# A decode-attention kernel: the token mixer moved to GpSimd and spread over the head groups, the x layouts made from one row, the last chunk loaded step by step

## The chip, the cores and the metric

The kernel runs on one core of one Trainium2 chip. The metric is the device time of one execution in microseconds (us), lower is better; the profile's span is about 1.8 us shorter than this time (1303.5 against 1305.27 us for the profiled run of the kernel before). The program is on one core, so there is no second die to compare, and only fast runs are compared (a single run, whose state is unknown, is marked). The granted clock is the share of TensorE's full clock that the profile shows for a stretch.

## The reference, cut to what matters

One query token attends to a long cache. There are 16 query heads in 8 groups, 65536 keys of 256 numbers for each group, in bf16, so K and V together are 537 MB that have to be read once. Beside it runs a small token mixer (layer norm, a product that makes 1792 x 448 numbers, gelu, a sum back to 448), and a sigmoid gate mixes both.

```python
q = (x @ wq).reshape(B, Sq, 16, 256) ...          # x: 1 x 448
scores = einsum("bhqd,bhkd->bhqk", q, k) * (Dh ** -0.5)
o = einsum("bhqk,bhkd->bhqd", softmax(scores), v)  # then @ wo
u = gelu(einsum("bsd,sf->bdf", layernorm(x), w1) + b1)   # F = 1792
y = einsum("bdf,fs->bds", u, w2) + b2
return g * a + (1 - g) * b                         # g = sigmoid(sum(x * gate_w))
```

## The kernel before

K and V come in chunks of 4 MB (128 partitions x 32 KB) into a ring of five slots. A chunk is worked off in four steps, 256 steps in all. In a step, TensorE turns 1 MB of K in two halves, VectorE copies each half out of PSUM (where the results of TensorE's matmuls lie), TensorE makes scores, ScalarE takes exp, VectorE turns p, and four steps later TensorE multiplies p with V. The ring slot is then free and its next load is issued. The mixer rides along in the first head group, one block of 128 rows in every two steps.

```python
def mixer_mid(b):
    nc.vector.tensor_scalar(out=t_b[:], in0=t_b[:], scalar1=GELU_C1, scalar2=1.0, ...)   # L266
    nc.vector.tensor_tensor(out=t_b[:], in0=t_b[:], in1=u_b[:], op=ALU.mult)             # L269
    nc.scalar.activation(out=t_b[:], in_=t_b[:], func=ACT.Tanh, scale=GELU_C0)           # L270

def mixer_close(b):
    nc.vector.scalar_tensor_tensor(out=gel[:], in0=t_b[:], scalar=1.0, in1=u_b[:], ...)  # L273
    nc.tensor.matmul(y_ps, lhsT=w2T[:, b:b + 1], rhs=gel[:], ...)                        # L276
# ... cut: mixer_open makes u_b on VectorE (L260) and the square on ScalarE (L257)

for n in range(n_steps + LAG):          # LAG = 4
    transposes(n, 0); scores(n - 1); transposes(n, 1); p_transpose(n - 1)   # bounds cut
    mixer(n)                            # even n: close(b - 1), open(b); odd n: mid(b)
    epilogue(n)
    p_v(n - LAG)
    # ... cut: load the next K and V into the slots that are free now
```

In the timelines below each engine works its instructions in the order of the program. In an even step TensorE meets the matmul of `gel` directly after VectorE has been told to make `gel`, and VectorE does that only after the step's copies and the p transpose.

The x layouts before the change are several loads: `xa` (128 x 3), `xb` (2 x 64 x 1), the same for the gate weights, and a broadcast `xB` (128 x 448).

The softmax here doesn't subtract the row's maximum and nothing guards it: scores larger than these inputs give would overflow.

Of the kernel before, what the change touches and what calls it, by code (L numbers as in the profile page):

```python
# [8 lines left out]
FP32 = mybir.dt.float32  # L9
BF16 = mybir.dt.bfloat16  # L10
ACT = mybir.ActivationFunctionType
ALU = mybir.AluOpType
AXIS = mybir.AxisListType
# [3 lines left out]
DH = 256  # L17


NB = 64  # L20
CHUNK = 128 * NB

SB = 16
STEPS = NB // SB
RING = 5

LAG = 4
NPT = LAG + 2

GELU_C0 = 0.7978845608028654  # L30
GELU_C1 = 0.044715
# [3 lines left out]
def kernel(  # L35
# [15 lines left out]
    nc = tc.nc  # L51
    D = A_x.shape[-1]
    SK = A_k_cache.shape[2]
    F = B_w1.shape[-1]
    NF = F // 128
    KA = D // 128
    DA = KA * 128
# [3 lines left out]
    steps_g = n_chunks * STEPS  # L61
    n_steps = HKV * steps_g
    assert steps_g >= LAG + 4
    scale = 1.0 / (DH ** 0.5)
# [3 lines left out]
    const = ctx.enter_context(tc.tile_pool(name="const", bufs=1))  # L68
    ringp = ctx.enter_context(tc.tile_pool(name="ring", bufs=1))
    work = ctx.enter_context(tc.tile_pool(name="work", bufs=1))  # L70
    psum = ctx.enter_context(tc.tile_pool(name="psum", bufs=1, space=bass.MemoryType.PSUM))

    ring = [ringp.tile([128, NB * DH], BF16, name=f"ring{i}") for i in range(RING)]

    tps = [psum.tile([128, 8 * 128], FP32, name=f"tps{i}") for i in range(2)]
    sc = [psum.tile([128, 512], FP32, name=f"sc{i}") for i in range(2)]
    pv = psum.tile([128, 512], FP32, name="pv")
    misc = psum.tile([128, 512], FP32, name="misc")


    total = HKV * n_chunks
    LAST_K = [SB] * STEPS
    LAST_V = [2 * SB, SB, SB // 2 + 2, SB // 2 - 2]

    def load(item):
        i, is_v = divmod(item, 2)
        g, c = divmod(i, n_chunks)
        src = (A_v_cache if is_v else A_k_cache)[0, g, c * CHUNK:(c + 1) * CHUNK, :]
        src = src.rearrange("(p j) d -> p (j d)", j=NB)
        dst = ring[item % RING]  # L90
        parts = [NB]
        if i == total - 1:
            parts = LAST_V if is_v else LAST_K
        j = 0
        for n in parts:
            nc.sync.dma_start(out=dst[:, j * DH:(j + n) * DH], in_=src[:, j * DH:(j + n) * DH])
            j += n
# [4 lines left out]
    wqb = wq_slot[:, KA * HQ * DH:KA * HQ * DH + 8 * DH]  # L102
# [3 lines left out]
    for hh in range(2):  # L106
        nc.sync.dma_start(
            out=wqb[64 * hh:64 * hh + 64, :], in_=A_wq[DA:D, 8 * DH * hh:8 * DH * (hh + 1)]
        )
# [4 lines left out]
    xa = const.tile([128, KA], BF16)  # L114
    xb = const.tile([128, 2], BF16)
    gwa = const.tile([128, KA], BF16)
    gwb = const.tile([128, 1], BF16)
    nc.vector.memset(xb[:], 0.0)
    nc.vector.memset(gwb[:], 0.0)
    x_row = A_x[0, 0]  # L120
    nc.scalar.dma_start(out=xa[:], in_=x_row[0:DA].rearrange("(p k) -> p k", k=KA))
    for hh in range(2):
        nc.scalar.dma_start(
            out=xb[64 * hh:64 * hh + 64, hh:hh + 1], in_=x_row[DA:D].rearrange("(p o) -> p o", o=1)
        )
    nc.gpsimd.dma_start(out=gwa[:], in_=gate_w[0:DA].rearrange("(p k) -> p k", k=KA))
    nc.gpsimd.dma_start(out=gwb[0:64, :], in_=gate_w[DA:D].rearrange("(p o) -> p o", o=1))

    xB = work.tile([128, D], FP32, name="xB")
    nc.gpsimd.dma_start(out=xB[:], in_=x_row.partition_broadcast(128))  # L130
# [20 lines left out]
    ones_f = const.tile([128, 128], FP32)  # L151
    nc.gpsimd.memset(ones_f[:], 1.0)


    sel = const.tile([128, 2, 2], FP32)
    same = const.tile([128, 4, 32], FP32)
    nc.gpsimd.memset(sel[:], 0.0)
    nc.gpsimd.memset(same[:], 0.0)
    for a in range(4):
        nc.gpsimd.affine_select(  # L160
            out=sel[:].rearrange("p h r -> p (h r)"), in_=sel[:].rearrange("p h r -> p (h r)"),
            compare_op=ALU.not_equal, fill=1.0, base=-32 * a, pattern=[[-1, 4]],
            channel_multiplier=1,
        )
        for half in range(16):
            nc.gpsimd.affine_select(
                out=same[:, :, 2 * half:2 * half + 2], in_=same[:, :, 2 * half:2 * half + 2],
                compare_op=ALU.not_equal, fill=1.0, base=-32 * a, pattern=[[0, 4], [-16, 2]],
                channel_multiplier=1,
            )  # L170

# [8 lines left out]
    acc = work.tile([1, D], FP32, name="acc")  # L180
    res = work.tile([1, D], BF16, name="res")
# [4 lines left out]
    nc.vector.memset(pv[:], 0.0)  # L186


    xg = const.tile([128, KA + 1], FP32)
    nc.vector.tensor_tensor(out=xg[:, 0:KA], in0=xa[:], in1=gwa[:], op=ALU.mult)  # L190
    nc.vector.tensor_tensor(out=xg[:, KA:KA + 1], in0=xb[:, 0:1], in1=gwb[:], op=ALU.mult)
    xg1 = const.tile([128, 1], FP32)
    nc.vector.tensor_reduce(out=xg1[:], in_=xg[:], axis=AXIS.X, op=ALU.add)
    z_ps = misc[:, 500:501]
    nc.tensor.matmul(z_ps, lhsT=ones_f[:], rhs=xg1[:], start=True, stop=True)
# [5 lines left out]

    stats = const.tile([128, nc.vector.BN_STATS_DIM], FP32)
    nc.vector.bn_stats(out=stats[:], in_=xB[:])
# [4 lines left out]
    mhalf = const.tile([128, 1], FP32)  # L208
    nc.gpsimd.memset(mhalf[:], -0.5)
# [3 lines left out]
    for _ in range(2):  # L213
# [6 lines left out]
    h_bc = xB  # L220
    nc.vector.tensor_scalar(
        out=h_bc[:], in0=xB[:], scalar1=mv[:, 0:1], scalar2=rstd[:, 0:1],
# [7 lines left out]
    for c in range(2):  # L230
        for h in range(HQ):
            dst = q_ps[:, c * HQ + h:c * HQ + h + 1]
            for k in range(KA):
                nc.tensor.matmul(
                    dst, lhsT=wqa_v[:, k, h, :, c], rhs=xa[:, k:k + 1], start=(k == 0), stop=False
                )
            nc.tensor.matmul(
                dst, lhsT=wqb_v[:, h % 8, :, c], rhs=xb[:, h // 8:h // 8 + 1],
                start=False, stop=True,
            )  # L240
# [10 lines left out]
    y_ps = misc[0:1, 0:D]  # L251
    u_b = work.tile([128, D], FP32, name="u_b")
    t_b = work.tile([128, D], FP32, name="t_b")
    gel = work.tile([128, D], BF16, name="gel")

    def mixer_open(b):
        nc.scalar.activation(  # L257
            out=t_b[:], in_=h_bc[:], func=ACT.Square, scale=w1T[:, b:b + 1], bias=b1T[:, b:b + 1]
        )
        nc.vector.tensor_scalar(  # L260
            out=u_b[:], in0=h_bc[:], scalar1=w1T[:, b:b + 1], scalar2=b1T[:, b:b + 1],
            op0=ALU.mult, op1=ALU.add,
        )

    def mixer_mid(b):
        nc.vector.tensor_scalar(  # L266
            out=t_b[:], in0=t_b[:], scalar1=GELU_C1, scalar2=1.0, op0=ALU.mult, op1=ALU.add
        )
        nc.vector.tensor_tensor(out=t_b[:], in0=t_b[:], in1=u_b[:], op=ALU.mult)  # L269
        nc.scalar.activation(out=t_b[:], in_=t_b[:], func=ACT.Tanh, scale=GELU_C0)  # L270

    def mixer_close(b):
        nc.vector.scalar_tensor_tensor(  # L273
            out=gel[:], in0=t_b[:], scalar=1.0, in1=u_b[:], op0=ALU.add, op1=ALU.mult
        )
        nc.tensor.matmul(  # L276
            y_ps, lhsT=w2T[:, b:b + 1], rhs=gel[:], start=(b == 0), stop=(b == NF - 1)
        )

    def mixer_end():  # L280
        nc.vector.tensor_scalar(
            out=acc[:], in0=y_ps, scalar1=0.5, scalar2=b2[0:1, 0:1], op0=ALU.mult, op1=ALU.add
        )
        nc.vector.tensor_scalar(
            out=acc[:], in0=acc[:], scalar1=gate[0:1, 1:2], scalar2=None, op0=ALU.mult
        )

    mix_pitch = max(1, min(2, (steps_g + LAG - 2) // (NF + 1)))

    def mixer(n):  # L290
        if mix_pitch == 1:
            if n < NF:
                mixer_open(n)
                mixer_mid(n)
                mixer_close(n)
            if n == NF:
                mixer_end()
            return
        b, ph = divmod(n - 2, 2)
        if ph == 0:  # L300
            if 0 < b <= NF:
                mixer_close(b - 1)
            if b == NF:
                mixer_end()
            if 0 <= b < NF:
                mixer_open(b)
        elif 0 <= b < NF:
            mixer_mid(b)
# [47 lines left out]
    def den_tot(g):  # L356
        d_ps = misc[:, 501:502]
        nc.tensor.matmul(
            d_ps, lhsT=same[:].rearrange("p a m -> p (a m)"), rhs=dsum[:], start=True, stop=True
        )  # L360
        nc.vector.reciprocal(out=rden[:], in_=d_ps)
        nc.vector.tensor_tensor(out=rden[:], in0=rden[:], in1=gate[:, 0:1], op=ALU.mult)
# [6 lines left out]
    def o_turn(g):  # L369
        o_ps = misc[:, 504:508]  # L370
        for c in range(2):
            for half in range(2):
                lo = half * DH + c * 128
                nc.tensor.matmul(
                    o_ps[:, 2 * c:2 * c + 2], lhsT=pvs[:, lo:lo + 128], rhs=sel[:, half, :],
                    start=(half == 0), stop=(half == 1),
                )
        nc.vector.tensor_copy(out=oT[:], in_=o_ps)
# [85 lines left out]
```

## Time and profile before

| | before |
|---|---|
| time, median of the first 3 runs | 1303.32 us (1302.59 to 1304.16) |
| span of the profiled run | 1303.5 us |
| DMA rate, 112 to 230 us | 363 GB/s |
| DMA rate, 230 to 430 us | 432 GB/s |
| landing of the last-but-one K chunk | 1266.4 us |

The page's first two parts. Tenths and rates stand in 40 equal slices of the span, 32.6 us each.

```profile
PE 962.2 (74%) x8448; PEld 600.4 (46%) x8448; DVE 810.3 (62%) x897; ACT 194.7 (15%) x543; POOL 22.7 (2%) x94
...
DMA  9998889999999999999999999999999999999995
GB/s 358 428 421 377 370 354 383 430 432 429 430 432 431 432 433 433 431 432 431 431 433 429 432 432 430 432 430 434 431 432 432 430 433 432 432 433 431 429 429 251
```

No compute engine is near full over the span, and the loads run at 430 to 434 GB/s nearly everywhere. The exceptions are what can be won: the first slice, slices four to seven, and the end. The same in stretches of the span (length, busy time and instructions of each engine, granted clock, DMA share, GB/s; PE is TensorE and PEld its weight loads, DVE VectorE, ACT ScalarE, POOL GpSimd):

```profile
core 0: us, PE busy (x) PEld busy (x) DVE busy (x) ACT busy (x) POOL busy (x), PEclk, DMA share, GB/s
65.00:112.00 47.00, 34.32 (x260) 20.61 (x260) 31.65 (x41) 10.40 (x24) 0.00 (x0) 0.78 1.00 427
112.00:230.00 118.00, 92.19 (x760) 56.27 (x760) 84.55 (x108) 25.61 (x62) 0.00 (x0) 0.83 0.87 363
230.00:430.00 200.00, 149.60 (x1306) 93.18 (x1304) 121.75 (x128) 27.51 (x80) 1.50 (x2) 0.85 1.01 432
630.00:1030.00 400.00, 299.14 (x2627) 186.56 (x2626) 246.03 (x261) 55.71 (x162) 2.25 (x3) 0.85 1.00 432
```

From 112 to 230 us the DMA engines are busy only 0.87 of the time. The waits between 65 and 230 us (who waited for whom, total, times, longest) name the mixer, and the timeline (start, length, what) shows how:

```profile
ACT t_b L270 <- DVE t_b L269: 41.4, 12, 4.0
PE misc L276 <- DVE gel L273: 40.7, 13, 3.1
DVE kT_326 L317 <- PE tps_74 L316: 34.5, 14, 2.8
```

```profile
153.73 1.09 PE L316 MATMUL tps_75<-ident,ring_69 128*128 128x128 f32 x8
...
154.43 1.22 DVE L317 COPY kT_325<-tps_74 128x2048 bf16<-128x2048 bf16 x1
...
155.56 1.21 DVE L317 COPY kT_325<-tps_75 128x2048 bf16<-128x2048 bf16 x1
156.69 0.70 DVE L338 STREAM_TRANSPOSE pT_332<-p_328 128x512 bf16<-128x512 bf16 x1
157.32 0.58 DVE L273 SCALAR_TENSOR_TENSOR gel<-t_b,u_b 128x448 bf16<-128x448 f32 x1
157.93 0.51 DVE L260 TENSOR_SCALAR u_b<-xB,w1T,b1T 128x448 f32<-128x448 f32 x1
157.95 0.53 PE L276 MATMUL misc<-gel,w2T 128*1 128x448 bf16 x1 [3.13 <-DVE gel L273]
...
159.27 1.97 PE L316 MATMUL tps_74<-ident,ring_69 128*128 128x128 f32 x8
...
161.27 1.22 DVE L317 COPY kT_326<-tps_74 128x2048 bf16<-128x2048 bf16 x1 [2.83 <-PE tps_74 L316]
```

TensorE stands still for 3.13 us until `gel` is there. Only then does it turn the next K half, and VectorE in its turn stands still for 2.83 us. The two engines take turns instead of overlapping. From one matmul of `gel` to the next it is 11.0 to 12.4 us, while the 4 MB of a pair come every 9.8 us (half of the 19.67 us between K chunks later on). So ring slots come free too late, and the loads have to wait for them.

The end is another matter. In the chain of work that ended last, the last-but-one K chunk lands at 1242.58 + 23.80 = 1266.4 us; from there eight steps of 3.13 us and the closing arithmetic take 37 us:

```profile
1242.58 23.80 DMA ring_73<-in_A_k_cache_dram
```

### The profile page before, as it was taken

The page shows a single profiled execution, that of the slowest core. Times are in us where ns is not written, and L with a number is a line of the kernel's source. Part 1 is how long each engine was busy: PE and PEld are TensorE (multiplying, and loading weights), DVE is VectorE, ACT ScalarE, POOL GpSimd, SP SyncE. Part 2 cuts the span into 40 slices and gives each one's busy share as a digit, 9 for nine tenths or more (in the row PEclk, how much of TensorE's full clock was granted, in tenths as well). Part 3 has the DMA queues.
Part 4 walks back from the last instruction along what each step waited for, and adds up shares of the span by engine and source line. Part 5 has one row for each costly group of instructions (what it writes and reads, how often), then busy time and mean ns, then how long its engine had stood idle before and what let it go on. Part 6 is the DMA issues. An engine that isn't in the chain of part 4 may idle for free.

```text
span 1303.5 us, 19519 instructions
## 1 busy us (share of the span) xinstructions
PE 962.2 (74%) x8448; PEld 600.4 (46%) x8448; DVE 810.3 (62%) x897; ACT 194.7 (15%) x543; POOL 22.7 (2%) x94
## 2 busy tenths in 40 slices
PE   3577778776777876867876876867877867868778
PEld 2344445444444444544544544544544544445444
DVE  2666668655655756656656656646556646657557
ACT  0122221111111111111111111111111111111111
POOL 5000000000000000000000000000000000000000
PEclk9777789888978878888888888889888878888889
DMA  9998889999999999999999999999999999999995
GB/s 358 428 421 377 370 354 383 430 432 429 430 432 431 432 433 433 431 432 431 431 433 429 432 432 430 432 430 434 431 432 432 430 433 432 432 433 431 429 429 251
DMA packets 21575, 545.71 MB, mean 419 GB/s; under 512 B 3057, under 2 KB 3314, under 8 KB 4466
## 3 DMA queue, kind: packets, MB, share of 16 engines
q1 hardware_dynamic: 19602, 540.55, 96.9%
q0 software_dynamic: 1584, 3.92, 0.8%
q8 instruction: 66, 1.08, 0.3%
q14 instruction: 19, 0.16, 0.0%
q10 hardware_dynamic: 304, 0.00, 0.0%
HBM read 544.34 MB, written 0.00 MB: 418 GB/s over the span
## 4 chain that ended last, share of the span: by engine, by line
DMA 54%; PE 38%; DVE 7%; issue 1%; ACT 0%; ACTq 0%
PE tps_74 L316 13%; PE tps_75 L316 12%; DMA ring_71<-in_A_k_cache_dram 12%; DMA ring_73<-in_A_k_cache_dram 12%; DMA ring_69<-in_A_k_cache_dram 11%; DMA ring_70<-in_A_k_cache_dram 10%; DMA ring_72<-in_A_k_cache_dram 9%; PE pv L348 6%; PE sc_77 L326 3%; PE sc_76 L326 3%; DVE kT_325 L317 2%; DVE kT_326 L317 1%; DMA xa<-in_A_x_dram 1%; DVE t_b L269 1%; DVE gel L273 1%
## 5 line engine op out<-in xcount | busy, mean ns | idle before, releaser
L317 DVE COPY kT_325<-tps_74 128x2048 bf16<-128x2048 bf16 x128 | 154.8, 1209 | 302.2 <-PE tps_74 L316 302.2
L317 DVE COPY kT_325<-tps_75 128x2048 bf16<-128x2048 bf16 x128 | 156.6, 1224 | 85.6 <-PE tps_75 L316 85.0
L317 DVE COPY kT_326<-tps_74 128x2048 bf16<-128x2048 bf16 x128 | 153.2, 1197 | 43.8 <-PE tps_74 L316 42.8
L317 DVE COPY kT_326<-tps_75 128x2048 bf16<-128x2048 bf16 x128 | 156.8, 1225 | 36.3 <-PE tps_75 L316 36.2
L332 ACT ACTIVATE p_328<-sc_77 128x512 bf16<-128x512 f32 x128 | 76.2, 595 | 620.5 <-PE sc_77 L326 620.5
L332 ACT ACTIVATE p_327<-sc_76 128x512 bf16<-128x512 f32 x128 | 76.4, 597 | 385.4 <-PE sc_76 L326 385.4
L316 PE MATMUL tps_74<-ident,ring_71 128*128 128x128 f32 x416 | 69.8, 322 | 66.3 <-DMA ring_71<-in_A_k_cache_dram 66.3
L316 PE MATMUL tps_74<-ident,ring_69 128*128 128x128 f32 x416 | 67.8, 316 | 58.5 <-DMA ring_69<-in_A_k_cache_dram 58.5
L316 PE MATMUL tps_74<-ident,ring_73 128*128 128x128 f32 x416 | 69.2, 320 | 53.3 <-DMA ring_73<-in_A_k_cache_dram 53.3
L326 PE MATMUL sc_77<-kT_326,qT 128*32 128x512 bf16 x1024 | 101.6, 481 | 1.2 <-DVE kT_326 L317 1.2
L316 PE MATMUL tps_74<-ident,ring_70 128*128 128x128 f32 x416 | 67.0, 313 | 48.0 <-DMA ring_70<-in_A_k_cache_dram 48.0
L316 PE MATMUL tps_74<-ident,ring_72 128*128 128x128 f32 x384 | 63.6, 319 | 49.0 <-DMA ring_72<-in_A_k_cache_dram 49.0
L316 PEld LDWEIGHTS tps_74<-ident,ring_71 128*128 128x128 f32 x416 | 55.5, 165 | 92.1 <-issue 92.1
L316 PEld LDWEIGHTS tps_74<-ident,ring_69 128*128 128x128 f32 x416 | 54.0, 161 | 81.4 <-issue 72.3
L316 PEld LDWEIGHTS tps_74<-ident,ring_73 128*128 128x128 f32 x416 | 54.8, 163 | 78.5 <-issue 77.6
L316 PEld LDWEIGHTS tps_74<-ident,ring_70 128*128 128x128 f32 x416 | 53.1, 160 | 72.6 <-issue 72.2
L316 PEld LDWEIGHTS tps_74<-ident,ring_72 128*128 128x128 f32 x384 | 50.5, 164 | 72.5 <-issue 70.4
L326 PE MATMUL sc_76<-kT_325,qT 128*32 128x512 bf16 x1024 | 83.2, 402 | 0.2
L316 PE MATMUL tps_75<-ident,ring_71 128*128 128x128 f32 x416 | 65.1, 306 | 0.0
L316 PE MATMUL tps_75<-ident,ring_73 128*128 128x128 f32 x416 | 64.7, 306 | 0.0
L316 PEld LDWEIGHTS tps_75<-ident,ring_73 128*128 128x128 f32 x416 | 51.7, 157 | 28.0 <-issue 28.0
L316 PEld LDWEIGHTS tps_75<-ident,ring_71 128*128 128x128 f32 x416 | 51.6, 157 | 27.9 <-issue 27.9
(125 smaller groups left out, 951.6 us busy)
## 6 DMA issues: line engine op xcount, KB each, us to landing
ring_69<-in_A_k_cache_dram SPq DMA_DIRECT2D x13, 4096.0 KB, 24.0
ring_70<-in_A_v_cache_dram SPq DMA_DIRECT2D x13, 4096.0 KB, 33.2
ring_71<-in_A_k_cache_dram SPq DMA_DIRECT2D x13, 4096.0 KB, 24.1
ring_72<-in_A_v_cache_dram SPq DMA_DIRECT2D x13, 4096.0 KB, 33.7
ring_73<-in_A_k_cache_dram SPq DMA_DIRECT2D x13, 4096.0 KB, 25.0
ring_69<-in_A_v_cache_dram SPq DMA_DIRECT2D x13, 4096.0 KB, 33.6
ring_70<-in_A_k_cache_dram SPq DMA_DIRECT2D x12, 4096.0 KB, 24.4
ring_71<-in_A_v_cache_dram SPq DMA_DIRECT2D x12, 4096.0 KB, 33.5
```

The lines of the kernel that those rows point to most:

```text
L269: nc.vector.tensor_tensor(out=t_b[:], in0=t_b[:], in1=u_b[:], op=ALU.mult)
L273: nc.vector.scalar_tensor_tensor(out=gel[:], in0=t_b[:], scalar=1.0, in1=u_b[:], op0=ALU.add, op1=ALU.mult)
L316: nc.tensor.transpose(tp[:, 128 * jj:128 * jj + 128], kn[:, j0 + jj, :], ident[:])
L317: nc.vector.tensor_copy(out=kT[n % 2][:, 8 * DH * half:8 * DH * (half + 1)], in_=tp[:].bitcast(BF16))
L326: nc.tensor.matmul(sc[n % 2][32 * a:32 * a + 32, :], lhsT=qT[:, c, g].rearrange("p r x -> p (r x)"), rhs=kv[:, :, 32 * a:32 * a + 32, c], ...
L332: nc.scalar.activation(out=p_t[n % 2][:], in_=sc[n % 2][:], func=ACT.Exp, scale=scale, accum_out=den[g % 2][:, n % steps_g:n % steps_g + 1],)
L348: nc.tensor.matmul(pv[32 * a:32 * a + 4, :], lhsT=pT[:, i, :, 0], rhs=vt[:, j * DH:(j + 2) * DH], start=first and i < 4, stop=last and i > ...
```

## The change

It has three intents: take the mixer off VectorE and out of the first head group (a block now takes eight steps and reaches into several groups); load x once as a row and make all its layouts on TensorE; and load the last chunk in pieces of about one step, with the first piece of V ahead of the last piece of K (before, all of K came first, and V began with a piece of two steps). With the second intent the whole start-up was reworked: the constant masks are built with fewer GpSimd operations (GpSimd is busy for 18.2 us of the first 22 us before), and part of wq comes in one load instead of two.

```diff
-        for n in parts:
-            nc.sync.dma_start(...)              # last K in 4 pieces, then last V in 4
+        elif item == 2 * total - 1:
+            for it, j, n in (
+                (k, 0, SB), (k, SB, SB), (k, 2 * SB, SB), (v, 0, SB), (k, 3 * SB, SB),
+                (v, SB, SB), (v, 2 * SB, SB), (v, 3 * SB, SB - tail), (v, NB - tail, tail),
+            ):
+                piece(it, j, n)
... cut
-    xa = const.tile([128, KA], BF16)            # and xb, gwa, gwb, xB, five loads and a broadcast
+    x_row = const.tile([1, D], BF16)
+    nc.scalar.dma_start(out=x_row[:], in_=A_x[0])
+    gw_row = const.tile([1, D], BF16)
+    nc.scalar.dma_start(out=gw_row[:], in_=gate_w.rearrange("(o n) -> o n", o=1))
... cut: five matmuls with a one make xT from it, one more makes the broadcast in PSUM
-    mix_pitch = max(1, min(2, (steps_g + LAG - 2) // (NF + 1)))
+    MIX = min(8, (n_steps - LAG) // (NF + 1))
     def mixer(n):
+        b, ph = divmod(n - LAG, MIX)
+        if ph == 0:
+            nc.scalar.activation(out=t_b[:], ..., func=ACT.Square, ...)
+            nc.gpsimd.tensor_scalar(out=u_b[:], ...)
+            nc.gpsimd.tensor_scalar(out=t_b[:], in0=t_b[:], scalar1=GELU_C1, scalar2=1.0, ...)
+            nc.gpsimd.tensor_tensor(out=t_b[:], in0=t_b[:], in1=u_b[:], op=ALU.mult)
+        if ph == 2:
+            nc.scalar.activation(out=t_b[:], in_=t_b[:], func=ACT.Tanh, scale=GELU_C0)
+            nc.gpsimd.tensor_scalar(out=t_b[:], in0=t_b[:], scalar1=1.0, scalar2=None, op0=ALU.add)
+            nc.gpsimd.tensor_tensor(out=gel[:], in0=t_b[:], in1=u_b[:], op=ALU.mult)
+        if ph == 5:
+            nc.tensor.matmul(misc[0:1, 0:D], lhsT=w2T[:, b:b + 1], rhs=gel[:], start=True, stop=True)
+            nc.vector.scalar_tensor_tensor(out=acc[:], in0=misc[0:1, 0:D], ...)
```

More of the change, by code (lines that the diff above doesn't have):

```diff
@@ L81, with piece @@
     total = HKV * n_chunks
-    LAST_K = [SB] * STEPS
-    LAST_V = [2 * SB, SB, SB // 2 + 2, SB // 2 - 2]
-    def load(item):
+    def piece(item, j, n):
         i, is_v = divmod(item, 2)
@@ L89, in load @@
         src = src.rearrange("(p j) d -> p (j d)", j=NB)
-        dst = ring[item % RING]
-        parts = [NB]
-        if i == total - 1:
-            parts = LAST_V if is_v else LAST_K
-        j = 0
-        for n in parts:
-            nc.sync.dma_start(out=dst[:, j * DH:(j + n) * DH], in_=src[:, j * DH:(j + n) * DH])
-            j += n
+        nc.sync.dma_start(
+            out=ring[item % RING][:, j * DH:(j + n) * DH], in_=src[:, j * DH:(j + n) * DH]
+        )
+    def load(item):
+        if item < 2 * total - 2:
+            piece(item, 0, NB)
+        elif item == 2 * total - 1:
+            k, v = item - 1, item
+            tail = SB // 2 - 2
+            for it, j, n in (
[3 more added lines that the diff above has]
+                piece(it, j, n)
     wq_slot = ring[RING - 1]
@@ L105 @@
     )
-    for hh in range(2):
-        nc.sync.dma_start(
-            out=wqb[64 * hh:64 * hh + 64, :], in_=A_wq[DA:D, 8 * DH * hh:8 * DH * (hh + 1)]
-        )
+    nc.sync.dma_start(out=wqb, in_=A_wq[DA:D, :].rearrange("r (hh n) -> (r hh) n", hh=2))
     for item in range(RING - 1):
         load(item)
-    xa = const.tile([128, KA], BF16)
-    xb = const.tile([128, 2], BF16)
-    gwa = const.tile([128, KA], BF16)
-    gwb = const.tile([128, 1], BF16)
-    nc.vector.memset(xb[:], 0.0)
-    nc.vector.memset(gwb[:], 0.0)
-    x_row = A_x[0, 0]
-    nc.scalar.dma_start(out=xa[:], in_=x_row[0:DA].rearrange("(p k) -> p k", k=KA))
-    for hh in range(2):
-        nc.scalar.dma_start(
-            out=xb[64 * hh:64 * hh + 64, hh:hh + 1], in_=x_row[DA:D].rearrange("(p o) -> p o", o=1)
-        )
-    nc.gpsimd.dma_start(out=gwa[:], in_=gate_w[0:DA].rearrange("(p k) -> p k", k=KA))
-    nc.gpsimd.dma_start(out=gwb[0:64, :], in_=gate_w[DA:D].rearrange("(p o) -> p o", o=1))
-    xB = work.tile([128, D], FP32, name="xB")
-    nc.gpsimd.dma_start(out=xB[:], in_=x_row.partition_broadcast(128))
+    x_row = const.tile([1, D], BF16)
+    nc.scalar.dma_start(out=x_row[:], in_=A_x[0])
+    gw_row = const.tile([1, D], BF16)
+    nc.scalar.dma_start(out=gw_row[:], in_=gate_w.rearrange("(o n) -> o n", o=1))
     w1T = const.tile([128, NF], FP32)
@@ L150 @@
     make_identity(nc, ident[:])
-    ones_f = const.tile([128, 128], FP32)
-    nc.gpsimd.memset(ones_f[:], 1.0)
-    sel = const.tile([128, 2, 2], FP32)
-    same = const.tile([128, 4, 32], FP32)
+    sel = const.tile([128, 4], FP32)
+    pick = const.tile([128, 2], FP32)
+    same = const.tile([128, 64, 2], FP32)
     nc.gpsimd.memset(sel[:], 0.0)
-    nc.gpsimd.memset(same[:], 0.0)
-    for a in range(4):
-        nc.gpsimd.affine_select(
-            out=sel[:].rearrange("p h r -> p (h r)"), in_=sel[:].rearrange("p h r -> p (h r)"),
-            compare_op=ALU.not_equal, fill=1.0, base=-32 * a, pattern=[[-1, 4]],
-            channel_multiplier=1,
-        )
-        for half in range(16):
+    nc.gpsimd.memset(pick[:], 0.0)
+    for t, w, step in ((sel, 4, -1), (pick, 2, -16)):
+        for a in range(4):
             nc.gpsimd.affine_select(
-                out=same[:, :, 2 * half:2 * half + 2], in_=same[:, :, 2 * half:2 * half + 2],
-                compare_op=ALU.not_equal, fill=1.0, base=-32 * a, pattern=[[0, 4], [-16, 2]],
-                channel_multiplier=1,
-            )
+                out=t[:], in_=t[:], compare_op=ALU.not_equal, fill=1.0, base=-32 * a,
+                pattern=[[step, w]], channel_multiplier=1,
+            )
+    nc.gpsimd.tensor_copy(
+        out=same[:], in_=pick[:].rearrange("p (o r) -> p o r", o=1).to_broadcast([128, 64, 2])
+    )
+    mhalf = const.tile([128, 1], FP32)
+    nc.gpsimd.memset(mhalf[:], -0.5)
+    one_b = const.tile([1, 128], BF16)
+    nc.vector.memset(one_b[:], 1.0)
+    one_f = const.tile([1, 128], FP32)
+    nc.vector.memset(one_f[:], 1.0)
     kT = [work.tile([128, SB * DH], BF16, name=f"kT{i}") for i in range(2)]
@@ L180 @@
     acc = work.tile([1, D], FP32, name="acc")
+    half_g = work.tile([1, 1], FP32, name="half_g")
     res = work.tile([1, D], BF16, name="res")
@@ L186 @@
     nc.vector.memset(pv[:], 0.0)
-    xg = const.tile([128, KA + 1], FP32)
-    nc.vector.tensor_tensor(out=xg[:, 0:KA], in0=xa[:], in1=gwa[:], op=ALU.mult)
-    nc.vector.tensor_tensor(out=xg[:, KA:KA + 1], in0=xb[:, 0:1], in1=gwb[:], op=ALU.mult)
-    xg1 = const.tile([128, 1], FP32)
-    nc.vector.tensor_reduce(out=xg1[:], in_=xg[:], axis=AXIS.X, op=ALU.add)
+    nc.vector.memset(acc[:], 0.0)
+    xd = const.tile([1, 2, 128], BF16)
+    nc.vector.memset(xd[:], 0.0)
+    for hh in range(2):
+        nc.vector.tensor_copy(
+            out=xd[:, hh, :].rearrange("o (r two) -> o r two", two=2)[:, :, hh],
+            in_=x_row[:, DA:D],
+        )
+    x_ps = misc[:, 480:480 + KA + 2]
+    for k in range(KA + 2):
+        if k < KA:
+            row = x_row[:, 0:DA].rearrange("o (p k) -> o p k", k=KA)[:, :, k]
+        else:
+            row = xd[:, k - KA, :]
+        nc.tensor.matmul(x_ps[:, k:k + 1], lhsT=row, rhs=one_b[:, 0:1], start=True, stop=True)
+    xT = const.tile([128, KA + 2], BF16)
+    nc.vector.tensor_copy(out=xT[:], in_=x_ps)
+    u_b = work.tile([128, D], FP32, name="u_b")
+    xg = u_b[0:1, :]
+    nc.vector.tensor_tensor(out=xg, in0=x_row[:], in1=gw_row[:], op=ALU.mult)
+    z1 = const.tile([1, 1], FP32)
+    nc.vector.tensor_reduce(out=z1[:], in_=xg, axis=AXIS.X, op=ALU.add)
     z_ps = misc[:, 500:501]
-    nc.tensor.matmul(z_ps, lhsT=ones_f[:], rhs=xg1[:], start=True, stop=True)
+    nc.tensor.matmul(z_ps, lhsT=one_f[:], rhs=z1[:], start=True, stop=True)
     nc.scalar.activation(out=gate[:, 0:1], in_=z_ps, func=ACT.Exp, scale=-1.0)
@@ L199 @@
     nc.vector.reciprocal(out=gate[:], in_=gate[:])
+    xb_ps = sc[0][:, 0:D]
+    nc.tensor.matmul(xb_ps, lhsT=one_b[:], rhs=x_row[:], start=True, stop=True)
     stats = const.tile([128, nc.vector.BN_STATS_DIM], FP32)
-    nc.vector.bn_stats(out=stats[:], in_=xB[:])
+    nc.vector.bn_stats(out=stats[:], in_=xb_ps)
     mv = const.tile([128, nc.vector.BN_AGGR_DIM], FP32)
@@ L207 @@
     nc.vector.tensor_scalar(out=veps[:], in0=mv[:, 1:2], scalar1=1e-5, scalar2=None, op0=ALU.add)
-    mhalf = const.tile([128, 1], FP32)
-    nc.gpsimd.memset(mhalf[:], -0.5)
     rstd = const.tile([128, 1], FP32)
@@ L219 @@
         nc.vector.tensor_tensor(out=rstd[:], in0=rstd[:], in1=nt[:], op=ALU.mult)
-    h_bc = xB
+    h_bc = work.tile([128, D], FP32, name="h_bc")
     nc.vector.tensor_scalar(
-        out=h_bc[:], in0=xB[:], scalar1=mv[:, 0:1], scalar2=rstd[:, 0:1],
+        out=h_bc[:], in0=xb_ps, scalar1=mv[:, 0:1], scalar2=rstd[:, 0:1],
         op0=ALU.subtract, op1=ALU.mult,
@@ L234 @@
                 nc.tensor.matmul(
-                    dst, lhsT=wqa_v[:, k, h, :, c], rhs=xa[:, k:k + 1], start=(k == 0), stop=False
+                    dst, lhsT=wqa_v[:, k, h, :, c], rhs=xT[:, k:k + 1], start=(k == 0), stop=False
                 )
+            x_h = KA + h // 8
             nc.tensor.matmul(
-                dst, lhsT=wqb_v[:, h % 8, :, c], rhs=xb[:, h // 8:h // 8 + 1],
-                start=False, stop=True,
+                dst, lhsT=wqb_v[:, h % 8, :, c], rhs=xT[:, x_h:x_h + 1], start=False, stop=True
             )
@@ L248 @@
     load_wo(1)
-    y_ps = misc[0:1, 0:D]
-    u_b = work.tile([128, D], FP32, name="u_b")
     t_b = work.tile([128, D], FP32, name="t_b")
     gel = work.tile([128, D], BF16, name="gel")
-    def mixer_open(b):
-        nc.scalar.activation(
-            out=t_b[:], in_=h_bc[:], func=ACT.Square, scale=w1T[:, b:b + 1], bias=b1T[:, b:b + 1]
-        )
-        nc.vector.tensor_scalar(
-            out=u_b[:], in0=h_bc[:], scalar1=w1T[:, b:b + 1], scalar2=b1T[:, b:b + 1],
-            op0=ALU.mult, op1=ALU.add,
-        )
@@ L265, in mixer_mid @@
-    def mixer_mid(b):
-        nc.vector.tensor_scalar(
-            out=t_b[:], in0=t_b[:], scalar1=GELU_C1, scalar2=1.0, op0=ALU.mult, op1=ALU.add
-        )
-        nc.vector.tensor_tensor(out=t_b[:], in0=t_b[:], in1=u_b[:], op=ALU.mult)
-        nc.scalar.activation(out=t_b[:], in_=t_b[:], func=ACT.Tanh, scale=GELU_C0)
-    def mixer_close(b):
-        nc.vector.scalar_tensor_tensor(
-            out=gel[:], in0=t_b[:], scalar=1.0, in1=u_b[:], op0=ALU.add, op1=ALU.mult
-        )
-        nc.tensor.matmul(
-            y_ps, lhsT=w2T[:, b:b + 1], rhs=gel[:], start=(b == 0), stop=(b == NF - 1)
-        )
@@ L280, in mixer_end @@
-    def mixer_end():
-        nc.vector.tensor_scalar(
-            out=acc[:], in0=y_ps, scalar1=0.5, scalar2=b2[0:1, 0:1], op0=ALU.mult, op1=ALU.add
-        )
-        nc.vector.tensor_scalar(
-            out=acc[:], in0=acc[:], scalar1=gate[0:1, 1:2], scalar2=None, op0=ALU.mult
-        )
-    mix_pitch = max(1, min(2, (steps_g + LAG - 2) // (NF + 1)))
-    def mixer(n):
-        if mix_pitch == 1:
-            if n < NF:
-                mixer_open(n)
-                mixer_mid(n)
-                mixer_close(n)
-            if n == NF:
-                mixer_end()
+    MIX = min(8, (n_steps - LAG) // (NF + 1))
@@ L298, in mixer @@
+    def mixer(n):
+        b, ph = divmod(n - LAG, MIX)
+        if not 0 <= b < NF:
             return
-        b, ph = divmod(n - 2, 2)
         if ph == 0:
-            if 0 < b <= NF:
-                mixer_close(b - 1)
-            if b == NF:
-                mixer_end()
-            if 0 <= b < NF:
-                mixer_open(b)
-        elif 0 <= b < NF:
-            mixer_mid(b)
+            nc.scalar.activation(
+                out=t_b[:], in_=h_bc[:], func=ACT.Square, scale=w1T[:, b:b + 1],
+                bias=b1T[:, b:b + 1],
+            )
+            nc.gpsimd.tensor_scalar(
+                out=u_b[:], in0=h_bc[:], scalar1=w1T[:, b:b + 1], scalar2=b1T[:, b:b + 1],
+                op0=ALU.mult, op1=ALU.add,
+            )
+            nc.gpsimd.tensor_scalar(
+                out=t_b[:], in0=t_b[:], scalar1=GELU_C1, scalar2=1.0, op0=ALU.mult, op1=ALU.add
+            )
+            nc.gpsimd.tensor_tensor(out=t_b[:], in0=t_b[:], in1=u_b[:], op=ALU.mult)
+        if ph == 2:
+            nc.scalar.activation(out=t_b[:], in_=t_b[:], func=ACT.Tanh, scale=GELU_C0)
+            nc.gpsimd.tensor_scalar(
+                out=t_b[:], in0=t_b[:], scalar1=1.0, scalar2=None, op0=ALU.add
+            )
+            nc.gpsimd.tensor_tensor(out=gel[:], in0=t_b[:], in1=u_b[:], op=ALU.mult)
+        if ph == 5:
+            nc.tensor.matmul(
+                misc[0:1, 0:D], lhsT=w2T[:, b:b + 1], rhs=gel[:], start=True, stop=True
+            )
+            if b == 0:
+                nc.vector.tensor_scalar(
+                    out=half_g[:], in0=gate[0:1, 1:2], scalar1=0.5, scalar2=None, op0=ALU.mult
+                )
+                nc.vector.tensor_scalar(
+                    out=acc[:], in0=acc[:], scalar1=b2[0:1, 0:1], scalar2=gate[0:1, 1:2],
+                    op0=ALU.add, op1=ALU.mult,
+                )
+            nc.vector.scalar_tensor_tensor(
+                out=acc[:], in0=misc[0:1, 0:D], scalar=half_g[0:1, 0:1], in1=acc[:],
+                op0=ALU.mult, op1=ALU.add,
+            )
@@ L358, in den_tot @@
         nc.tensor.matmul(
-            d_ps, lhsT=same[:].rearrange("p a m -> p (a m)"), rhs=dsum[:], start=True, stop=True
+            d_ps, lhsT=same[:].rearrange("p o r -> p (o r)"), rhs=dsum[:], start=True, stop=True
         )
@@ L374, in o_turn @@
                 nc.tensor.matmul(
-                    o_ps[:, 2 * c:2 * c + 2], lhsT=pvs[:, lo:lo + 128], rhs=sel[:, half, :],
+                    o_ps[:, 2 * c:2 * c + 2], lhsT=pvs[:, lo:lo + 128], rhs=sel[:, 2 * half:2 * half + 2],
                     start=(half == 0), stop=(half == 1),
```

## The prediction

> **What bounds the kernel now.** Three stretches, by DMA rate per stretch of the span. From 230 to 1285 us the DMA engines are 100% busy at 431 GB/s; TensorE waits 4 to 6 us for the ring before each K chunk (groups of waits). From about 112 to 230 us the rate is only 368 GB/s: compute holds it up. The timeline shows why: the mixer runs one block per two steps on VectorE, and TensorE, in order, waits 3.13 us for `gel` in every pair (40.7 us in 13 waits), so a pair of steps takes 11 to 12 us against 6.26 us later and 9.8 us for its data at 431 GB/s. The ring is freed too late. Last, the tail: the last-but-one K chunk lands at 1266.5 us (chain of waits); eight steps of 3.13 us with TensorE full, then normalise, project and store: 37 us, compute-bound.
>
> **The change.** (1) VectorE loses 2.07 us of mixer per block (0.51+0.35+0.63+0.58, groups by line) and gets one 1-row accumulate, about 0.6 us. A block takes eight steps, so TensorE and ScalarE read what GpSimd began two or three steps earlier. Five GpSimd operations a block: the Trainium skill, "GPSIMD Engine Reference", Performance versus the Vector engine, has 4497 ns for a two-input fp32 operation of 2048 elements; scaled to 448, my estimate is 1 us each, 4 to 5 us a block, against 25 us or more available; no run here shows it yet. Contention: "SBUF — State Buffer", Who interferes with whom, says that a VectorE instruction with at most one SBUF input outside the two-port modes does not contend with GpSimd; the K copies read PSUM and the p transposes one input, so I expect 1.22 us and 0.70 us to stay.
> So the stretch before 230 us becomes DMA-bound. Its lost time: 65 to 230 us at a mean of 381 GB/s, 165*(1-381/431) = 19 us, all on the critical path, since everything after is DMA-bound until the tail.
> (2) x by one row load: removes some 450 descriptors of 2 to 6 bytes and a 224 KB broadcast. The q projection now ends at 21 us, but four ring slots are loading already, so an earlier q frees little. The first 22 us move 328 GB/s; fewer small packets may give 0 to 3 us.
> (3) The last chunk's order: the last K piece lands about 22 us after K of the chunk before, TensorE wants it at 23.4; the last V piece at 29 us, wanted at 30. Compute-bound either way: about 0.
>
> **Sum.** 1303.3 - 19 - 2 = 1282 us. Cross-check: K chunks land every 19.67 us in the DMA-bound part; from the third (68.2 us, less 1 to 2) 60 intervals end at 1247, plus 37 of tail: 1284. Range 1276 to 1290. Faster by over 2% (under 1277): 0.15; within: 0.83; slower: 0.02.
>
> **What would show it.** Right: 425 to 432 GB/s in every slice but the first and last; TensorE's waits for `gel` near zero; last-but-one K near 1246; tail of 36 to 38 us; GpSimd busy 60 to 90 us more. Wrong: copies well over 1.22 us while GpSimd is busy, TensorE or ScalarE waiting for GpSimd tiles, the rate below 420 somewhere.
>
> **What would make it wrong.** GpSimd operations several times dearer, so that ScalarE's in-order tanh holds back the next exp; the freed time lost again to the ring; or the tail gaining (from 1285 to 1295 us DMA runs at half rate, some engines done early).

## The result, and the profile after

| | before | after |
|---|---|---|
| time, median | 1303.74 us (4 runs) | 1289.36 us (4 runs, 1289.0 to 1291.2) |
| ratio after/before | | 0.9894, 95% interval 0.9876 to 0.9911 |
| DMA rate, 112 to 230 us | 363 GB/s | 430 GB/s |
| DMA rate, 630 to 1030 us | 432 GB/s | 430 GB/s |
| last-but-one K chunk lands | 1266.4 us | 1249.7 us |

A ratio is the mean time of one kernel's fast runs over that of the other's of the same rounds, so not quite the ratio of the medians that are quoted. The change wins 14.4 us, about two thirds of the 21.3 us that the prediction gave. The page, the stretches and the chain of the kernel after:

```profile
PE 952.5 (74%) x8454; PEld 595.9 (46%) x8454; DVE 792.6 (62%) x859; ACT 193.2 (15%) x543; POOL 80.2 (6%) x101
...
DMA  9999999999999999999999999999999999999995
GB/s 392 431 430 433 427 432 425 429 432 429 433 425 433 429 431 428 429 430 429 432 429 426 433 430 430 430 430 427 435 427 433 425 430 431 430 430 418 436 421 241
```

```profile
core 0: us, PE busy (x) PEld busy (x) DVE busy (x) ACT busy (x) POOL busy (x), PEclk, DMA share, GB/s
65.00:112.00 47.00, 37.27 (x323) 22.92 (x323) 29.70 (x32) 7.99 (x22) 4.88 (x5) 0.84 1.01 431
112.00:230.00 118.00, 88.07 (x773) 55.37 (x773) 73.59 (x81) 19.50 (x53) 15.47 (x16) 0.84 1.00 430
230.00:430.00 200.00, 150.57 (x1326) 93.44 (x1328) 125.72 (x134) 33.41 (x92) 25.22 (x26) 0.85 1.00 430
630.00:1030.00 400.00, 298.02 (x2633) 186.54 (x2631) 247.33 (x263) 55.73 (x162) 2.31 (x3) 0.85 1.00 430
```

```profile
1226.33 23.41 DMA ring_73<-in_A_k_cache_dram
```

The hole from 112 to 230 us is gone: DMA share 1.00, 430 GB/s. None of the 14 matmuls of `gel` waits in this trace; what TensorE waits for between 65 and 230 us is now the loads:

```profile
PE tps_74 L315 <- DMA ring_72<-in_A_k_cache_dram: 10.6, 2, 5.6
```

After these waits TensorE is slow (eight transposes take 1.94 us at 143.03 us, after a wait of 5.01 us), but here the loads set the pace, so it costs nothing.

The tail from the landing on is 1287.6 - 1249.7 = 37.9 us, against 37.1 before. But there is something that nothing in the change should touch. From 630 to 1030 us, where the mixer is long over, the loads run at 430 instead of 432 GB/s. K chunks land every 19.75 us (64.83 us for the third chunk to 1249.74 us, 60 chunks) instead of every 19.67 us. Over 60 chunks that is 5 us, most of what is missing.

GpSimd's groups of instructions (busy us, mean ns of one, idle before):

```profile
L287 POOL TENSOR_SCALAR t_b<-t_b 128x448 f32<-128x448 f32 x14 | 18.6, 1328 | 61.4 <-ACT t_b L286 61.4
L290 POOL TENSOR_TENSOR gel<-t_b,u_b 128x448 bf16<-128x448 f32 x14 | 16.0, 1141 | 1.2
L284 POOL TENSOR_TENSOR t_b<-t_b,u_b 128x448 f32<-128x448 f32 x14 | 15.9, 1136 | 1.2
L277 POOL TENSOR_SCALAR u_b<-h_bc,w1T,b1T 128x448 f32<-128x448 f32 x14 | 10.0, 715 | 5.3 <-DMA b1T<-in_B_b_dram 3.9
L281 POOL TENSOR_SCALAR t_b<-t_b 128x448 f32<-128x448 f32 x14 | 7.9, 564 | 410.8 <-ACT t_b L273 410.8
```

They sum to 4.9 us a block, as estimated (two-input operations 1.14 us each, against the estimate of 1 us). VectorE's copies still take 1.19 to 1.22 us and its transposes 0.70 us, so the trace agrees with the Trainium skill, "SBUF — State Buffer", Who interferes with whom: no contention is seen (that the copies run outside the two-port modes, as its rule asks, the trace does not show). It is not seen where the two meet either: from 65 us on, the 55 copies that overlap one of these GpSimd operations take 1.21 us on average, as do the 441 others.

### The profile page after: what moved, and what is told of

The parts are those of the page before. It is cut to its first block, busy times and chain, and to the rows that moved or that the text cites. A ratio compares the mean times of both kernels' runs of the same rounds, so it can differ in the third digit from the quotient of the medians.

```text
span 1287.6 us, 19500 instructions
## 1 busy us (share of the span) xinstructions
PE 952.5 (74%) x8454; PEld 595.9 (46%) x8454; DVE 792.6 (62%) x859; ACT 193.2 (15%) x543; POOL 80.2 (6%) x101
## 4 chain that ended last, share of the span: by engine, by line
DMA 62%; PE 37%; DVE 1%; issue 0%; ACT 0%; SPq 0%; ACTq 0%; DVEq 0%
DMA ring_73<-in_A_k_cache_dram 15%; PE tps_74 L315 12%; DMA ring_69<-in_A_k_cache_dram 12%; DMA ring_72<-in_A_k_cache_dram 12%; PE tps_75 L315 12%; DMA ring_71<-in_A_k_cache_dram 12%; DMA ring_70<-in_A_k_cache_dram 11%; PE pv L347 6%; PE sc_77 L325 4%; PE sc_76 L325 3%; DMA ring_73<-in_A_wq_dram 1%; PE misc L292 0%; PE misc L247 0%; DVE kT_142 L316 0%; PE misc L357 0%
```

## The experiments

Two questions: what removed the hole, and why are all loads of the kernel after 0.4 per cent slower? The kernel before was run again (medians of 1304.7, 1305.4 and 1305.4 us in the experiments, each on another chip).

### Controls: both kernels unchanged

> Control: the kernel before, unchanged, for a second trace. Between 230 and 1230 us the first trace moved 431.4 GB/s and landed a K chunk every 19.67 us; the trace after moved 429.5 and landed one every 19.75 us. If this 0.4 per cent is the run's own scatter, this trace may show anything from 19.65 to 19.78; if it comes from the change, it shows 19.67 again. Time 1303 us.

> Control: the kernel after, unchanged. 1289 us. If the slower pace of 19.75 us a K chunk belongs to the change it is seen again here, beside 19.67 in the trace of before of the same chip.

Measured: before 1303.86 us (one run, so its state is unknown), its trace 432 to 433 GB/s between 730 and 1030 us and a K chunk every 19.66 us from 263 us on; after 1290.97 us (1289.72 to 1291.08), 429 to 430 GB/s there and a K chunk every 19.74 us, ratio 0.9893. The slower pace is no scatter: it belongs to the change.

### The change without its mixer

```diff
 # in the kernel after:
-    def mixer(n): ... GpSimd, eight steps a block
+    def mixer(n): ... as in the kernel before: VectorE, two steps a block
```

> The change without its mixer: VectorE mixer of two steps a block in the first head group, new x layouts and new tail kept. Theory (the gain is the stretch that the in-order mixer held up): back to the kernel before less the startup gain of about 3 us, 1298 to 1302 us, DMA at about 370 GB/s from 112 to 230 us, TensorE waiting 40 us for gel. Rival (the gain comes from the x layouts and the tail): stays at 1289 to 1293.

Measured: 1308.52 us (1307.57 to 1308.99), ratio 1.0029 (1.0014 to 1.0044), so slower than the kernel before. The stretches and the wait:

```profile
112.00:230.00 118.00, 92.98 (x773) 56.54 (x772) 86.50 (x109) 24.95 (x62) 0.75 (x1) 0.84 0.87 363
...
630.00:1030.00 400.00, 297.97 (x2626) 185.68 (x2618) 246.64 (x262) 55.77 (x162) 2.25 (x3) 0.85 1.00 429
```

```profile
PE misc L288 <- DVE gel L285: 37.5, 12, 3.1
```

The hole is back in full, and the theory's 1298 to 1302 us was missed. The new mixer is worth 1308.52 - 1290.97 = 17.5 us. And the rest of the change, alone, loses 1308.5 - 1304.7 = 3.8 us, which I had expected to win 3. The 429 GB/s is there without the new mixer, so the mixer is not what slows the loads.

### The mixer spread, but on VectorE

```diff
-            nc.gpsimd.tensor_scalar(...)      # all five mixer operations
+            nc.vector.tensor_scalar(...)
```

> The change with the five mixer operations on VectorE instead of GpSimd, still spread over eight steps a block. Theory (spreading and reading late is what counts, not the engine): VectorE has slack of several us in each eight steps, so 1288 to 1291 us, the same as after. Rival (VectorE's load was the limit, GpSimd is needed): several us slower, 1294 or more, DMA below 425 GB/s while the mixer lasts.

Measured: 1289.62 us (1289.33 to 1290.0), the same as after. GpSimd is not needed:

```profile
112.00:230.00 118.00, 90.16 (x790) 55.89 (x789) 80.85 (x97) 20.07 (x55) 0.75 (x1) 0.87 1.00 430
```

```profile
137.25 0.63 DVE L290 TENSOR_TENSOR gel<-t_b,u_b 128x448 bf16<-128x448 f32 x1
...
150.98 0.35 PE L292 MATMUL misc<-gel,w2T 128*1 128x448 bf16 x1
```

`gel` is ready 13 us before TensorE asks for it, and TensorE does not wait.

### The mixer on GpSimd, but not spread

```diff
-    MIX = min(8, (n_steps - LAG) // (NF + 1))      # phases 0, 2, 5 of 8
+    MIX = 2      # even step: matmul of block b-1, then open b; odd step: tanh and gel of b
```

> The kernel after with the mixer on GpSimd, but at the old pitch: one block every two steps, matmul and accumulate one phase after the tanh, all in the first head group. Theory (reading late is what counts, not the engine): five GpSimd operations take 4.9 us, with the two activations 6.2 us in a chain, and TensorE meets the result at the next step's start, so the hold-up comes back: 1297 to 1310 us, DMA below 410 GB/s between 112 and 230 us. Rival (taking the load off VectorE is what counts): 1289 to 1293.

Measured: 1290.17 us (1289.08 to 1291.3). My expectation missed; the hole stays closed:

```profile
112.00:230.00 118.00, 88.75 (x780) 55.67 (x782) 75.85 (x85) 23.30 (x59) 32.58 (x33) 0.84 1.00 429
```

```profile
133.84 1.14 POOL L309 TENSOR_TENSOR gel<-t_b,u_b 128x448 bf16<-128x448 f32 x1
...
135.22 0.35 PE L269 MATMUL misc<-gel,w2T 128*1 128x448 bf16 x1
```

In this block `gel` (ready at 133.84 + 1.14 = 134.98 us) comes 0.24 us before TensorE's turn, with no wait shown for it (in the next block it is 5.7 us). One step of distance between making `gel` and reading it is already enough with GpSimd. Moving the mixer to GpSimd with that one step, or spreading it on VectorE, wins all that the mixer had to give; GpSimd without the step was not run. Both versions have two things in common: `gel` is read at least one step after the step that makes it, and VectorE has less mixer work per step. Which of the two suffices by itself would take a version on VectorE, at the old pitch, that reads `gel` one step late. It was not run, so this stays open. The waits of the kernel before speak for the distance (a pair has 4 x 1.22 + 2 x 0.70 + 2.07 = 8.4 us of VectorE work, less than the 9.8 us of its data), but that is an argument, not a run. So does the spread version on VectorE: the step that opens a block has 0.47 + 0.39 + 0.63 = 1.49 us of mixer work there, more than the 0.58 + 0.51 = 1.09 us of an even step before, and yet TensorE's waits for VectorE's copies sum to 7.5 us from 65 to 230 us, against 40.7 us for `gel` before.

### Where the ring lies in SBUF

The slow loads are in every version with the new x layouts and in none with the old. Of the trace's DMA packet records, those of 32768 bytes (one partition's row of a chunk) between 300 and 700 us:

```
kernel            ring starts at   mod 256   packets   mean ns   packets of exactly 1213 ns
before            26880            0         5230      1216.05   5055
after             29344            160       5204      1220.63   632
```

The start addresses are those of the built programs. The new tiles of the start-up sit in front of the ring, and moved it from a multiple of 256 bytes to 160 bytes past one. The Trainium skill, "DMA: Bandwidth & Descriptors", How a descriptor splits into AXI transactions, says that when a descriptor does not start on a 256-byte boundary, its first transaction starts at the boundary below and the unused bytes are fetched and paid for, counted in beats of 32 bytes. It speaks of reading; that the SBUF side that a load writes behaves in the same way is an assumption made here. Counted in this way, 160 bytes in front of a 32 KB row are 5 beats on 1024, or 0.49 per cent: theory A, and the beats in the expectations below are this count. To test it, unused bytes were put in front of the ring, and no instruction of the loop was changed:

```diff
+    pad = const.tile([128, 48], BF16)      # 96 bytes: ring at 29440. 64: 29472, 32: 29408, 80: 29504
+    nc.vector.memset(pad[:], 0.0)
```

> The kernel after with 96 unused bytes a partition in front of the ring, so that the ring starts at a multiple of 256 bytes in SBUF, as it did before the change (26880; after: 29344, which is 160 past a multiple of 256). Theory A (the new x layout moved the ring; a 32 KB row that starts 160 bytes past a 256-byte boundary costs 5 more beats of 32 bytes in 1024, 0.49 per cent of the pace): 1283 to 1285 us, DMA 431 to 433 GB/s between 230 and 1230 us. Rival B (the pace has another cause in the new startup): stays at 1289 to 1291, 430 GB/s.

> As the run before but 128 bytes of padding: the ring starts 32 bytes past a multiple of 256. Theory A, counted in wasted beats: 1 beat in 1024, 1285 to 1286 us. Rival C (any start off a 64-byte boundary costs the same): 1289 to 1291, like the kernel after. Rival B: 1289 to 1291.

> As the run before but 64 bytes of padding: the ring starts 224 bytes past a multiple of 256. Theory A: 7 beats in 1024, 1292 to 1293 us. Rivals B and C: 1289 to 1291.

After these three had come back, one more:

> The kernel after with 160 bytes of padding: the ring starts 64 bytes past a multiple of 256. Starts at 32, 160 and 224 past 256 all cost the same, and all are 32 off a 64-byte boundary. If the unit is 64 bytes: 1283 to 1285 us and packets of 1213 ns, as with a multiple of 256. If it is 256 (or 128) bytes: 1289 to 1292 and packets of 1214 to 1226 ns.

Measured, with the packets of 300 to 700 us (after_mod64 and after_again are from other calls than the rest, so their ratios compare better than their times):

```
run            mod 256   time us, median (range)        ratio to before   packet mean ns   most frequent ns
after_align    0         1283.73 (1283.33 to 1285.71)   0.9838            1216.14          1213 (5036 of 5222)
after_mod32    32        1290.40 (1290.30 to 1290.59)   0.9886            1221.82          1216 (2737 of 5200)
after_mod64    64        1289.25 (1289.14 to 1289.56)   0.9880            1220.84          1215 (2557 of 5203)
after_again    160       1290.97 (1289.72 to 1291.08)   0.9893            1220.69          1214 (1527 of 5205)
after_mod224   224       1291.01 (1290.97 to 1292.35)   0.9894            1221.83          1216 (2722 of 5200)
```

The stretches and the chain of the aligned kernel:

```profile
112.00:230.00 118.00, 89.03 (x774) 56.16 (x774) 73.74 (x81) 19.65 (x53) 15.53 (x16) 0.84 1.01 432
230.00:430.00 200.00, 151.70 (x1346) 93.72 (x1345) 127.67 (x137) 34.08 (x94) 25.31 (x26) 0.86 1.00 432
630.00:1030.00 400.00, 297.80 (x2606) 186.05 (x2602) 245.48 (x260) 55.17 (x160) 2.31 (x3) 0.85 1.00 431
```

```profile
1220.49 23.79 DMA ring<-in_A_k_cache_dram
```

Rival B falls: 96 unused bytes win 5.6 to 7.2 us (against 1289.36 and 1290.97 us of the kernel after), the packets are back at 1213 ns, and the last-but-one K chunk lands at 1244.3 us. That the start address is the cause is shown, with one limit: the pad moves all tiles behind it by the same amount, those that VectorE and TensorE use too, and no run moves the ring alone. But it is the load packets that got shorter, and they write the ring; VectorE's copies take 1.21 us with and without the pad. Theory A falls in its amount: 32 bytes cost as much as 160 or 224, not a fifth of it. Rival C (a 64-byte boundary is enough) falls too, by the run at 64. What the runs say is: a start at a multiple of 256 bytes is good, starts at 32, 64, 160 and 224 past it all cost 5.5 to 7.3 us of 1284. Whether a multiple of 128 is enough was not tried. Why one loses about the same at every offset is not settled either: a cost paid once for each row that starts off such a boundary would look like this, but no run tests it. The aligned kernel beats both kernels.

### The old x layouts with the new mixer and tail

```diff
 # in the kernel before: the new mixer and the new tail put in, x layouts left as they were
```

> The kernel before with the new mixer and the new tail, but the old x layouts; the ring stands at 26880 as before (a multiple of 256). Theory A: the pace of before, 431 to 433 GB/s, and only the startup is lost, about 3 us against the aligned kernel after: 1286 to 1288, so faster than the kernel after although it has less of the change. Rival (the x layouts are a plain gain): 1291 to 1294.

Measured: 1286.26 us (1285.98 to 1286.79), ratio 0.9855, packets 1216.13 ns, ring at 26880. As expected, it is faster than the complete change. Against the aligned kernel the new x layouts, with the rest of the reworked start-up, are worth 1286.26 - 1283.73 = 2.5 us. The first 22 us move 385 GB/s in the aligned kernel and 343 here; (385 - 343) * 22 / 431 = 2.1 us, so most of it is there. Against the kernel before of this call, the new mixer and the new tail win 1305.4 - 1286.26 = 19.1 us.

### The old order of the last loads

```diff
 # in the aligned kernel: load() of the kernel before put back
```

> The aligned kernel after (1283.7 us) with the last two loads in the old order. Theory (the tail is bounded by TensorE from the landing of the last-but-one K chunk on): 1283 to 1285, same. Rival (the new order saves time): 1286 or more.

Measured: 1284.08 us (1283.39 to 1285.63), ratio 0.9841 (0.9824 to 0.9859) against 0.9838 (0.9823 to 0.9853) of the aligned kernel. The new order is worth nothing that these runs can see. It is bounded by TensorE from the landing of the last-but-one K chunk, as predicted.

### The mixer nearly left out

```diff
-        if not 0 <= b < NF:
+        if not 0 <= b < 1:      # one block of 14; the result is wrong on purpose
```

> The aligned kernel after with 13 of the 14 mixer blocks left out (a wrong result on purpose), to see what the mixer still costs. Theory (nothing, all hidden behind the loads): 1283 to 1285. Rival (GpSimd or the extra ScalarE and TensorE work still costs): 1281 or less.

Measured: 1285.6 us (1284.09 to 1286.37), a little above the range that was expected, ratio 0.985 (0.9832 to 0.9868) against 0.9841 of the aligned kernel with the old tail; the span of its fastest run is 1281.7 us beside 1281.6 of the aligned kernel. It is not faster, so nothing is left to win from the mixer.

## Why the prediction was right or wrong

The measured 1289.36 us lies in the range of 1276 to 1290, at its edge, and in the class "within 2%". That it still lies inside is luck: a cost of 5.5 to 7.3 us that no term foresaw just fits into the width of the range. Point by point:

- *What bounds the kernel.* Right. The hole of 112 to 230 us was the in-order wait for `gel`: with the old mixer it returns with the same 363 GB/s and a wait of the same 3.1 us. One link was short: a wait of 3.13 us on top of 6.26 us does not make the "11 to 12 us" of a pair. The rest is TensorE at a granted clock of 0.50 after the wait.
- *"19 us, all on the critical path".* Right: 17.5 us in the complete change (1308.52 to 1290.97), and 19.1 us with the tail when the x layouts stay as they were (1305.4 to 1286.26). It did become DMA time at the full rate, and the next wait was the ring.
- *GpSimd at 4 to 5 us a block, no contention.* Right: 4.9 us, copies and transposes unchanged. GpSimd was busy 57.5 us more (80.2 - 22.7), just under the 60 given. The reason given, that results are read two or three steps later, is more than is needed: one step later suffices on GpSimd, and spreading suffices on VectorE.
- *"0 to 3 us" for the x layouts, 2 in the sum.* This is the step that failed, by its sign. The layouts themselves won 2.5 us. But I counted only what their loads and instructions cost, and not that their tiles lie in front of the ring. By moving it off a multiple of 256 bytes, they made the 32 KB packets 4.5 to 5.7 ns longer on average (from 1216.1 ns to between 1220.6 and 1221.8 ns). The K and V loads are some 128 x 128 such packets, 1024 for each of the 16 DMA engines if they share evenly; by this estimate that is 4.6 to 5.8 us over the run, and the runs measured 5.5 to 7.3 us. So instead of the 2 us won of the sum, this step lost 3 to 5 us net.
- *The cross-check of "19.67 us" a K chunk.* It assumed that the pace of the loads is a constant of the chip. It was 19.75 us in the kernel after, and (1244.28 - 65.04) / 60 = 19.65 us in the aligned one. The last-but-one K chunk came at 1249.7 us instead of "near 1246"; aligned, at 1244.3. That sum was in units of the span, too, and the time is 1.8 us longer.
- *Tail: about 0.* Right: 1284.08 against 1283.73 us.
- *The sign "rate below 420 somewhere".* It was met once, by one slice of 418 GB/s (1159 to 1191 us) next to one of 436. Over both slices it is 427 GB/s at a DMA share of 1.00, so no hold-up stands behind it.

The sum with the measured terms: 1303.7 - 17.5 - 2.5 + 6.4 - 0.3 = 1289.8 us, where 6.4 is the middle of the alignment's cost and 0.3 the difference of the tail runs, which is no more than noise. Measured: 1289.4. The terms come from different calls, whose medians of the kernel before differ by 2 us, so a match to 0.4 us is in part luck.

## What to carry to other kernels

When an engine reads what another has just been told to make, in the same step, both can end up taking turns, as here; look for a wait of constant length in every step, and look at the granted clock after it (here 0.50), for the wait can cost more than its length. Try a step of distance between making and reading before you worry about which engine does the work: both versions that had it lost the wait, though no run tried the distance by itself. In a kernel that is bound by loads, check where the destination buffers lie: small tiles in front of them can move them, and here 96 unused bytes were worth more than the whole reworking of the layouts. When the pace of a stretch changes that the edit does not touch, take it as a finding and not as scatter: repeat both kernels and look at the durations of single packets.

## What the Trainium skill lacked or had wrong

- "DMA: Bandwidth & Descriptors", How a descriptor splits into AXI transactions, counts unused beats below a 256-byte boundary. It has nothing on what an SBUF destination off such a boundary costs in a load. Here packets of 32 KB took 1216.1 ns on average with the ring at a multiple of 256 bytes, and 1220.6 to 1221.8 ns at 32, 64, 160 and 224 bytes past it: 0.4 to 0.5 per cent, nearly the same for all, where the page's count would give 1 to 7 beats of 1024.
- "SBUF — State Buffer", Operand start alignment, says which starts are correct, and says nothing of the time that they cost: 1283.73 us with the ring aligned, 1289.25 to 1291.01 us without.
- "GPSIMD Engine Reference", Engine selection, calls one-input work roughly line-rate. In the kernel after a `tensor_scalar` of 128x448 with two constants took 564 ns, and one with a single constant (`scalar2=None`) 1328 ns, longer than a two-input operation (1136 ns); on VectorE, in the run with the mixer spread there, the same two took 387 and 351 ns. Whether the constants or the different operation (add alone, not multiply and add) makes the difference was not tried. No page has this.
- "DMA: Bandwidth & Descriptors", Latency and other measured facts, has DMA engines 7 and 15 as usually slower, and as its best guess ties this to DMAs issued from GpSimd. It has nothing on a larger group of late engines. Here the loads are issued from SyncE, and late in the traces of before and after, of the 16 completions that a load posts, seven come first and the last nine follow some 5 us later in a group; the spread between first and last is 2 us at 300 us of the kernel before and 10.8 us at 1225 us. Which engines these are, and why, the trace does not tell. It shows as half the rate in the last 10 us of loading (230 GB/s from 1285 to 1295 us before).
